# One array for a batch's attention inputs, turned memory summaries for batch 0, weight steps ahead of the last softmax steps

## The chip, the cores and the metric

The kernel runs on one core of a Trainium2 chip. The metric is the device time of one launch in microseconds (us); the time before is the median of three runs. A profiled execution gives the trace that is read here. Its engines are TensorE (PE for products, PEld for weight loads), VectorE (DVE), ScalarE (ACT), GpSimd (POOL) and SyncE (SP, which issues most of the loads).

## The reference

Three stages follow each other, all in float32:

- attention through memories, for 4 batches and 8 heads: with phi [576, 32] a softmax of phi over the 576 positions gives `a`; the summaries are `k_m = a^T k` and `v_m = a^T v` (32 x 64 each); then `softmax(q k_m^T / 8) v_m` over the 32 memories;
- a gated layer on the 2304 tokens of width 512: `(silu(x w_gate) * (x w_val)) w_out`, with 1536 inner columns;
- a layer of 8 experts with noisy top-2 routing and 1024 inner columns each.

The change touches the first stage for batch 0 (its input layout for all batches) and the first steps of the second stage.

## The kernel before

The program is one hand-ordered instruction stream for each engine (`manual_schedule`). Each engine runs its own instructions in the order in which the code names them and waits where its operands aren't there. The 2304 tokens are worked in 8 blocks of 288; a batch is two blocks. The 1536 inner columns of the second stage are 12 columns of 128, and a slot (`slot1`, or `slot0` for block 0) does one column of one block: gate and value products (`gv`, L436), the gate on VectorE (`gate_act`), the product back (`down`).

What comes before the first slot is the front. It is written out call by call (L735 to L776) for batch 0, in two halves of four heads each (`g` = 0, 1):

- `s1_a`, `s1_e`, `s1_r` (L248 to L260): maximum of phi, exponential with its sum, reciprocal of the sum (`st[:, 2]`).
- `s1_b`, `s1_bc` (L264 to L279): PE turns the exponentials in chunks of 128 positions (six transposes), ScalarE copies them to `en`.
- `s1_c` (L281): 20 calls of P.matmul for one summary, k or v of one half: five chunks by four heads, each head with an output of 32 memories by 64, the four on different output rows. `s1_cv` scales by the reciprocal, `s1_d` turns the result with PE, `s1_dc` copies it to `KM`.
- `s2_first` (L333): the first scores of one half and VectorE's 32x32 transposes of them; `s2_a` (maximum, subtract), `s2_e` (exponential, ScalarE), `s2_b` (sum, reciprocal, multiply, transpose), `s2_c` and `s2_d` (x's high part on ScalarE, its low part on VectorE).
- The second stage's weights come in thirds of 512 KB (`wa`). `top(n)` on ScalarE and `low(n)` on VectorE unpack third `n`, and `low` frees a buffer, for which SP then issues another load (L196). Thirds 0 and 1 are gate and value of column 0.
- The v summary is not applied to each token. `proj_a`, `proj_h`, `proj_b` (L397 to L413) multiply it into the weights of a column instead: PE's product, its high part on ScalarE, its low part on VectorE. `gv` multiplies high by high, low by high and high by low, for both halves: six products for the gate and six for the value.

SP's loads of the front stand in one queue: phi (two), k of half 0, q, k of half 1, v of both halves, then the thirds in the order of their use. PSUM tiles for small results take turns over six banks (`other`, L96).

Of the kernel before, what the change touches and what calls it, by code (L numbers as in the profile page):

```python
# [1 line left out]

# [57 lines left out]
OUT_ROWS = T + CAP  # L60


def r(ap):
    return ap.bitcast(F32R)
# [3 lines left out]
def moe_program(ctx, tc, phi, kv, q, wa, wgn, nz, wb, out):  # L68
# [41 lines left out]

    def load_phi(b, g):
        t = att.tile([128, S], F32, tag="phi", name="phi", bufs=2)
        Q.dma_start(t, phi[2 * b + g])
        PH[b, g] = t

    def load_part(s):
        for g in range(2):
            if s == 0:
                if g:
                    load_q(0)  # L120
                    KV[0, 1] = wpool.tile([128, 4096], F32, tag="X1", name="kv", bufs=1)[:, :2 * ROW].rearrange(
                        "p (s w) -> p s w", s=2)
                else:
                    KV[0, 0] = att.tile([128, 2, ROW], F32, tag="kv", name="kv", bufs=1)
            Q.dma_start(KV[0, g][:, s], kv[g, :, s])

    def load_kv(b, g):
        KV[b, g] = att.tile([128, 2, ROW], F32, tag="kv", name="kv", bufs=1)
        Q.dma_start(KV[b, g], kv[2 * b + g])

    def load_q(i):
        QT[i] = att.tile([128, 4, BT], F32, tag="q", name="qt", bufs=1)
        Q.dma_start(QT[i], q[i].rearrange("p (q t) -> p q t", q=4))
# [71 lines left out]
    for s in range(2):  # L205
        load_part(s)
# [56 lines left out]

    def s1_b(b, g):  # L264
        e, st = ST[b, g]
        p = other([128, 4, 128], "pT")
        for c in range(4):
            P.transpose(p[:, c, :], e[:, 128 * c:128 * (c + 1)], ident)
        p2 = other([128, 128], "pT")
        P.transpose(p2, e[:, S - 128:S], ident)  # L270
        P.transpose(p2[:64], e[:, S - 64:S], ident)
        TP[b, g] = p, p2
# [8 lines left out]
    def s1_c(b, g, s=slice(0, 2)):  # L281

        en, st = ST[b, g]
        p = other([128, 2, D] if b else [128, D], "pkv")
        t = KV[b, g][:, s]
        for c in range(5):
            for h in range(4):
                o, d = (slice(0, 128), 4 * D * c + D * h) if c < 4 else (
                    slice(64 * (h // 2), 64 * (h // 2) + 64), 16 * D + D * (h % 2))
                P.matmul(p[32 * h:32 * h + 32], en[o, c, 32 * h:32 * h + 32], t[o, ..., d:d + D],  # L290
                         start=(c == 0), stop=(c == 4))
        TP[b, g, s if b == 0 else 2] = p

    def s1_cv(b, g, s=2, eng=None):
        st = ST[b, g][1]
        out = kz[g][:, :, g, :] if s == 2 else kz[g][:, s, g, :]
        p = TP.pop((b, g, s))
        if eng is None:
            V.tensor_scalar(out, p, st[:, 2:3], None, op0=OP.mult)
        else:  # L300
            A.activation(out, p, AF.Copy, scale=st[:, 2:3])

    def s1_d(b, g, s=2):

        p = other([128, 2, 128], "pT")
        for m in range(2):
            if s in (m, 2):
                P.transpose(p[:64 * g + 64, m, :], kz[g][:, m].rearrange("p n d -> p (n d)"), ident)
        TP[b, g, s] = p

    def s1_dc(b, g, s=2):
        if b not in KM:
            KM[b] = att.tile([128, 2, 4, M], F32, tag="km", name="km", bufs=2)
        o = slice(64 * g, 64 * g + 64)
        m = slice(0, 2) if s == 2 else slice(s, s + 1)
        A.activation(KM[b][o, m].rearrange("p s k m -> p s (k m)"), TP.pop((b, g, s))[o, m], AF.Copy)
# [118 lines left out]

    def gv(i, f):  # L436
        pg, pv = bank(4, [128, BT], "pg"), bank(5, [128, BT], "pv")
        for a, p in enumerate((pg, pv)):
            for g in range(2):
# [307 lines left out]
    s1_cv(0, 1, 0, A)  # L747
    s2_e(0, 0)
    s1_d(0, 1, 0)
    s1_dc(0, 1, 0)  # L750
# [24 lines left out]
    del spare[:]  # L775
    spare.extend([6, 7])  # L776
# [44 lines left out]
    def slot0(f):  # L821
        run(0, 2 * f)
        c = ((f,) if f < 2 else (0, 1),)
        if f % 2 == 0 or f == 1:
            for fn in (proj_a, proj_h, proj_b):
                fn(0, f // 2, *c)
# [4 lines left out]
        if f == 0:  # L831
            top(2)
# [619 lines left out]
def layout(inputs):  # L1452
# [6 lines left out]
    arrays["phi"] = a("phi").reshape(B, 4, 2, S, M).transpose(0, 2, 1, 4, 3).reshape(2 * B, 128, S)  # L1459
    kv = np.stack([a("k").reshape(B, 4, 2, S, D), a("v").reshape(B, 4, 2, S, D)], axis=4)  # L1460
    kv = kv.transpose(0, 2, 3, 4, 1, 5).reshape(2 * B, S, 2, 4 * D)
    tail = kv[:, 512:].reshape(2 * B, 64, 2, 2, 2 * D).transpose(0, 3, 1, 2, 4).reshape(2 * B, 128, 2, 2 * D)
    kv = kv[:, :512].reshape(2 * B, 4, 128, 2, 4 * D).transpose(0, 2, 3, 1, 4).reshape(2 * B, 128, 2, 16 * D)
    arrays["kv"] = np.concatenate([kv, tail], axis=-1)
    q = a("q").reshape(B, 4, 2, S, D).transpose(1, 2, 4, 0, 3).reshape(4, 128, NB, BT)
    arrays["q"] = q.transpose(2, 1, 0, 3).reshape(NB, 128, 4 * BT)
# [17 lines left out]
_ORDER = ["phi", "kv", "q", "wa", "wgn", "nz", "wb"]  # L1484
# [15 lines left out]
```

## Time and profile before

| | |
|---|---|
| runs before | 847.76, 848.74, 850.28 us (median 848.74) |
| profiled execution | 849.52 us, span 847.7 us from first to last instruction |
| mean granted TensorE clock | 0.987 |
| busy, share of the span | PE 822.0 us (97%), PEld 729.4 (86%), DVE 638.7 (75%), ACT 389.9 (46%), POOL 247.5 (29%) |
| HBM | 105.34 MB read, 36.68 MB written, 168 GB/s over the span |

The span is the time between the first and the last instruction of the trace; the profiled execution's own time has 1.8 us around it. Engine busy time leaves out instructions that only wait, branch or issue a load. The granted clock is what the throttle allowed TensorE, as a share of 2.4 GHz; 0.50 is the lower of its two levels.

### The profile page before, as it was taken

Reading aid. Unit: us, or ns where it says so; the run is one execution under the profiler, and the core shown is the slowest. Engines: PE = TensorE matmul, PEld = TensorE weight load, DVE = VectorE, ACT = ScalarE, POOL = GpSimd, SP = SyncE. Lnnn points to the kernel's source line nnn. Section 1 sums busy time; section 2 is a strip of 40 time slices with the busy share of each in tenths; the row PEclk is TensorE's granted clock in tenths of the full one; section 3 lists DMA queues with packets and bytes.
Section 4 is the critical chain, followed back from the end, with each engine's and each line's share of the span. In section 5 each row is a group of like instructions: output and inputs, shape, how many; then the busy total and the mean of one; then the engine's idle time right before and its main releaser. Section 6 shows DMA issues by size and latency. Waiting matters only on the chain. (4 is left out here: it accounts for less than half of the span.)

```text
span 847.7 us, 16453 instructions
## 1 busy us (share of the span) xinstructions
PE 822.0 (97%) x6224; PEld 729.4 (86%) x6224; DVE 638.7 (75%) x1532; ACT 389.9 (46%) x804; POOL 247.5 (29%) x347
## 2 busy tenths in 40 slices
PE   5899999999999999999999999999999999999996
PEld 3678888899989998989899988888888888888885
DVE  4788497675867577777685587798889988899771
ACT  4665565333443334333445455445446464454430
POOL 2000012424333242443122143322414324054232
PEclk8799999999999999999999999999999999999999
DMA  9983838884426363446946993635574645654521
GB/s 341 402 328 125 254 98 303 262 279 131 124 51 214 99 207 98 131 112 145 272 151 222 211 254 73 136 111 115 138 172 87 161 116 119 163 117 108 182 82 64
DMA packets 78280, 143.18 MB, mean 169 GB/s; under 512 B 16080, under 2 KB 36784, under 8 KB 77424
## 3 DMA queue, kind: packets, MB, share of 16 engines
q1 hardware_dynamic: 58832, 100.66, 38.2%
q0 software_dynamic: 19360, 41.38, 20.1%
q8 instruction: 51, 0.84, 0.4%
q14 instruction: 37, 0.30, 0.1%
HBM read 105.34 MB, written 36.68 MB: 168 GB/s over the span
## 5 line engine op out<-in xcount | busy, mean ns | idle before, releaser
L1144 PE MATMUL acc<-ws,hs 128*128 128x512 f32 (+1 forms) x690 | 174.9, 394 | 0.0
L1130 PEld LDWEIGHTS ph<-xh,ws 128*128 128x128 f32 x1008 | 150.9, 188 | 11.0 <-DVE y L1170 0.8
L1130 PE MATMUL ph<-xh,ws 128*128 128x308 f32 x1008 | 157.6, 304 | 1.3 <-DVE y L1170 0.6
L1144 PEld LDWEIGHTS acc<-ws,hs 128*128 128x128 f32 (+1 forms) x690 | 122.7, 184 | 24.4
L985 POOL DMA_INDIRECT out<-pv,ix x40 | 64.2, 1606 | 179.9 <-ACT pv L977 70.8
L474 PE MATMUL acc<-a,ro 128*128 128x288 f32 x576 | 116.4, 295 | 0.0
L441 PE MATMUL pg<-x,pt 128*128 128x288 f32 x576 | 103.2, 314 | 4.4 <-DVE ta L454 2.3
L474 PE MATMUL acc<-a,os 128*128 128x288 f32 x432 | 105.8, 294 | 0.8 <-DVE os L423 0.8
L441 PEld LDWEIGHTS pg<-x,pt 128*128 128x128 f32 x576 | 82.1, 191 | 24.1 <-issue 6.8
L441 PE MATMUL pv<-x,pt 128*128 128x288 f32 x576 | 93.3, 298 | 0.0
L474 PEld LDWEIGHTS acc<-a,ro 128*128 128x128 f32 x576 | 92.1, 188 | 0.0
L441 PEld LDWEIGHTS pv<-x,pt 128*128 128x128 f32 x576 | 83.1, 191 | 0.0
L454 DVE SCALAR_TENSOR_TENSOR ta<-ta,pg 128x288 f32<-128x288 f32 x84 | 37.8, 450 | 60.1 <-ACT ta L449 60.1
L638 POOL DMA_INDIRECT xs<-R,gidx x48 | 48.2, 1004 | 112.6 <-DMA xs<-R,gidx 95.0
L474 PEld LDWEIGHTS acc<-a,os 128*128 128x128 f32 x432 | 74.1, 188 | 1.1 <-DVE os L423 1.1
L449 ACT ACTIVATE ta<-pg 128x288 f32<-128x288 f32 x84 | 34.4, 409 | 80.1 <-PE pg L441 80.1
L460 ACT ACTIVATE a<-ta 128x288 fp32r<-128x288 f32 x84 | 37.3, 444 | 70.6 <-DVE ta L455 66.9
L433 POOL DMA_DIRECT2D os<-osl x72 | 40.7, 567 | 93.5 <-PE acc L474 50.2
L942 PE MATMUL ph<-xt,wm 128*128 128x384 f32 (+1 forms) x256 | 55.6, 307 | 0.9 <-DVE xt L904 0.9
L942 PEld LDWEIGHTS ph<-xt,wm 128*128 128x128 f32 x256 | 43.8, 189 | 3.7 <-DVE xt L904 1.1
L455 DVE TENSOR_TENSOR ta<-ta,pv 128x288 f32<-128x288 f32 x84 | 38.2, 455 | 9.1 <-DVE ta L454 0.5
L461 DVE TENSOR_TENSOR a<-ta,a 128x288 fp32r<-128x288 f32 x84 | 37.5, 446 | 5.3 <-ACT a L460 4.9
(234 smaller groups left out, 1442.1 us busy)
## 6 DMA issues: line engine op xcount, KB each, us to landing
wb<-wb SPq DMA_DIRECT2D x70, 512.0 KB, 4.5
os<-osl POOLq DMA_DIRECT2D x72, 256.0 KB
kv<-kv SPq DMA_DIRECT2D x6, 1152.0 KB, 9.2
xl<-xs SPq DMA_DIRECT2D x40, 160.0 KB, 6.4
stg<-wa SPq DMA_DIRECT2D x12, 511.8 KB, 8.3
out<-zt SPq DMA_DIRECT2D x1, 5888.0 KB
xd<-R SPq DMA_DIRECT2D x8, 603.0 KB
qt<-q SPq DMA_DIRECT2D x8, 576.0 KB, 6.7
```

The costliest lines, as they stand in the source:

```text
L433: G.dma_start(r(lo), r(osl[f][:, :]))
L441: P.matmul(p, r(PT[f // 2, g][:, w, f % 2, 128 * a:128 * a + 128]), r(X[i][:, s, g, :]), start=(g == 0 and n == 0), stop=(g == 1 and n == 2))
L454: V.scalar_tensor_tensor(ta, ta, 1.0, pg, op0=OP.add, op1=OP.mult)
L455: V.tensor_mul(ta, ta, pv)
L460: A.activation(r(ah[:, 0, :]), ta, AF.Copy)
L461: V.tensor_sub(r(ah[:, 1, :]), ta, ah[:, 0, :])
L474: P.matmul(ACC[i][c], r(OS[i, f][w][:, o]), r(ah[:, s, :]), start=(f == 0 and n == 0), stop=(f == NF1 - 1 and n == 2))
L638: G.indirect_dma_start(out=xs[:, :], out_offset=bass.IndirectOffsetOnAxis(ap=RT[i][:, t, n:n + 1], axis=0), in_=R[i][:, t, :], in_offset=None)
L942: P.matmul(p, r(w[:, c]), r(x[:, k, b, :]), start=(m == 0), stop=(m == 11))
L985: G.indirect_dma_start(out=out, out_offset=bass.IndirectOffsetOnAxis(ap=IX[e][:h, t:t + 1], axis=0), in_=PV[e, t][:h], in_offset=None, com ...
L1130: P.matmul(out, r(w[i][:, c + 128 * k:c + 128 * k + 128]), r(x[:, m, k, a]), start=(start and n == 0), stop=(n == 5), skip_group_check=not ...
L1144: P.matmul(AC2[e, t][:h], r(a[:, n, o]), r(w[b][:, n]), start=(f == 0 and m == 0), stop=(f == NF2 - 1 and m == 2))
```

## The change

All of a batch's attention inputs lie in one array, `xin`, block after block in the order in which batch 0 loads them, each block contiguous over its 128 partitions. Later batches load k and v of a half by two loads. For batch 0 the reciprocal is multiplied into an identity (`dg`), and plain products with it turn and scale the exponentials in one step; `turned` then computes a summary directly in its turned form, 64 output rows (the width of a head) by 32 memories, two heads at a time side by side, and copies it to `KM` on ScalarE; the scale, PE's second transposes and their copies are gone for batch 0. The order of the front is written anew: the unpacking of thirds 0 to 2 and column 0's projection stand ahead of the last softmax steps, and x's low parts come last. The first gate and value products of block 0 take x's low part last (`FEW`). Block 0's softmax result of half 1 gets a place of its own in the tile that holds `dg`.

```diff
+PLACE, LONG = {}, 0
+for name, n in (("phi0", S), ("phi1", S), ("k0", 18 * D), ("q0", 4 * BT), ("k1", 18 * D), ("v0", 18 * D),
+                ("v1", 18 * D), ("q1", 4 * BT)):
+    PLACE[name] = LONG, n
+    LONG += 128 * n
...
+    def section(b, name):
+        o, n = PLACE[name]
+        return xin[b, o:o + 128 * n].rearrange("(p n) -> p n", n=n)
...
+    def load_part(b, g, s):
+        if (b, g) not in KV:
+            if b == 0 and g:
+                KV[b, g] = wpool.tile([128, 4096], F32, tag="X1", name="kv", bufs=1)[:, :2 * ROW].rearrange(
+                    "p (s w) -> p s w", s=2)
+            else:
+                KV[b, g] = att.tile([128, 2, ROW], F32, tag="kv", name="kv", bufs=1)
+        Q.dma_start(KV[b, g][:, s], section(b, f"{'kv'[s]}{g}"))
     def load_kv(b, g):
-        KV[b, g] = att.tile([128, 2, ROW], F32, tag="kv", name="kv", bufs=1)
-        Q.dma_start(KV[b, g], kv[2 * b + g])
+        for s in range(2):
+            load_part(b, g, s)
...
     load_phi(0, 1)
-    for s in range(2):
-        load_part(s)
+    load_part(0, 0, 0)
+    load_q(0)
+    for g, s in ((1, 0), (0, 1), (1, 1)):
+        load_part(0, g, s)
...
     def s1_b(b, g):
         e, st = ST[b, g]
+        if b:
+            turn = partial(P.transpose, identity=ident)
+        else:
+            if not EX:
+                EX.append(gpool.tile([128, 2, 2, BT], F32, tag="x", name="ex"))
+            dg = EX[0][:, 0, g, :128]
+            V.tensor_scalar(dg, ident, st[:, 2:3], None, op0=OP.mult)
+            turn = partial(P.matmul, rhs=dg, start=True, stop=True)
         p = other([128, 4, 128], "pT")
         for c in range(4):
-            P.transpose(p[:, c, :], e[:, 128 * c:128 * (c + 1)], ident)
+            turn(p[:, c, :], e[:, 128 * c:128 * (c + 1)])
         p2 = other([128, 128], "pT")
-        P.transpose(p2, e[:, S - 128:S], ident)
-        P.transpose(p2[:64], e[:, S - 64:S], ident)
+        turn(p2, e[:, S - 128:S])
+        turn(p2[:64], e[:, S - 64:S])
         TP[b, g] = p, p2
...
+    def turned(g, s):
+        en = ST[0, g][0]
+        z = slice(64 * g, 64 * g + 64)
+        for m in range(2):
+            p = other([128, 64], "pkv")
+            for n in range(2):
+                for c in range(5):
+                    o, d = (slice(0, 128), 4 * D * c + D * (2 * m + n)) if c < 4 else (
+                        slice(64 * m, 64 * m + 64), 16 * D + D * n)
+                    h = 64 * m + 32 * n
+                    P.matmul(p[z, 32 * n:32 * n + 32], KV[0, g][o, s, d:d + D], en[o, c, h:h + 32],
+                             start=(c == 0), stop=(c == 4))
+            A.activation(memory(0)[z, s, 64 * m:64 * m + 64], p[z], AF.Copy)
...
-        at = att.tile([128, BT], F32, tag="at", name="at")
+        at = att.tile([128, BT], F32, tag="at", name="at") if i or not g else EX[0][:, 1, 0, :]
...
+    ALL = [(w, s, g) for g in range(2) for w, s in ((0, 0), (0, 1), (1, 0))]
+    FEW = [(w, s, g) for w, s in ((0, 0), (1, 0), (0, 1)) for g in range(2)]
     def gv(i, f):
         pg, pv = bank(4, [128, BT], "pg"), bank(5, [128, BT], "pv")
         for a, p in enumerate((pg, pv)):
-            for g in range(2):
-                for n, (w, s) in enumerate(((0, 0), (0, 1), (1, 0))):
-                    P.matmul(p, r(PT[f // 2, g][:, w, f % 2, 128 * a:128 * a + 128]), r(X[i][:, s, g, :]),
-                             start=(g == 0 and n == 0), stop=(g == 1 and n == 2))
+            for n, (w, s, g) in enumerate(FEW if i == f == 0 else ALL):
+                P.matmul(p, r(PT[f // 2, g][:, w, f % 2, 128 * a:128 * a + 128]), r(X[i][:, s, g, :]),
+                         start=(n == 0), stop=(n == 5))
...
-    for fn in (s1_a, s1_e, s1_r):
+    for fn in (s1_a, s1_e):
         both(fn, 0)
     for g in range(2):
+        s1_r(0, g)
         s1_b(0, g)
         s1_bc(0, g)
-    s1_c(0, 0, 0)
-    s1_cv(0, 0, 0)
-    s1_d(0, 0, 0)
-    s1_dc(0, 0, 0)
+    turned(0, 0)
     s2_first(0)
     s2_a(0, 0)
-    s1_c(0, 1, 0)
-    s1_cv(0, 1, 0, A)
+    turned(1, 0)
     s2_e(0, 0)
-    s1_d(0, 1, 0)
-    s1_dc(0, 1, 0)
     s2_b(0, 0)
     s2_first(1)
     s2_a(0, 1)
-    s1_c(0, 0, 1)
-    s1_cv(0, 0, 1, A)
-    s1_d(0, 0, 1)
+    top(0)
+    low(0)
+    turned(0, 1)
     s2_c(0, 0)
-    s1_dc(0, 0, 1)
-    s2_d(0, 0)
-    s2_e(0, 1)
-    s1_c(0, 1, 1)
-    s1_cv(0, 1, 1, A)
-    s1_d(0, 1, 1)
-    s1_dc(0, 1, 1)
-    top(0)
-    s2_b(0, 1)
-    low(0)
-    s2_c(0, 1)
     top(1)
     low(1)
-    s2_d(0, 1)
+    s2_e(0, 1)
+    turned(1, 1)
     places(True)
+    del spare[:]
+    spare.extend([6, 7])
+    proj_a(0, 0, (0,))
+    top(2)
+    proj_h(0, 0, (0,))
+    s2_b(0, 1)
+    s2_c(0, 1)
+    proj_b(0, 0, (0,))
+    both(s2_d, 0)
...
-        if f % 2 == 0 or f == 1:
+        if f and f % 2 == 0 or f == 1:
...
-        if f == 0:
-            top(2)
```

## Rows read from the trace of the kernel before

**Rows 1.** The page: span, and 40 slices: PE's busy tenths, granted clock's tenths.

```profile
span 847.7 us, 16453 instructions
...
PE   5899999999999999999999999999999999999996
...
PEclk8799999999999999999999999999999999999999
```

**Rows 2.** Windows: stretch, length, busy (count) PE PEld DVE ACT POOL, clock, DMA, GB/s.

```profile
5.00:10.00 5.00, 4.27 (x52) 3.40 (x52) 0.80 (x6) 2.49 (x8) 0.63 (x1) 1.00 0.98 336
...
10.00:15.00 5.00, 3.25 (x58) 1.25 (x58) 2.83 (x8) 1.30 (x4) 0.00 (x0) 0.82 1.02 415
...
20.00:25.00 5.00, 1.95 (x19) 1.10 (x20) 2.51 (x5) 2.95 (x7) 0.00 (x0) 0.50 1.02 407
...
30.00:35.00 5.00, 5.00 (x47) 3.43 (x46) 3.22 (x7) 3.12 (x6) 0.00 (x0) 0.63 1.04 407
```

**Rows 3.** Order of time, first summaries: start, length, engine, line, operation, out<-in, count, [idle].

```profile
1.27 0.23 DVE L216 TENSOR_SCALAR ident<-jp 128x128 f32<-128x128 int32 x1 [1.27 <-POOL warm L220]
...
5.25 1.12 PE L268 MATMUL pT<-ident,phi 128*128 128x128 f32 x4 [5.25 <-ACT phi L255]
...
5.41 0.16 DVE L260 RECIPROCAL st<-st 128x1 f32<-128x1 f32 x1
...
8.33 1.45 PE L290 MATMUL pkv<-kv,en 128*32 128x64 f32 x40 [0.26 <-ACT en L277]
...
9.34 0.20 PEld L290 LDWEIGHTS pkv<-kv,en 64*32 64x32 f32 x8 [0.17 <-issue]
...
10.53 0.27 ACT L316 ACTIVATE km<-pT 64x128 f32<-64x128 f32 x1 [2.08 <-PE pT L308]
...
10.85 0.69 PE L326 MATMUL psc<-qt,km 64*32 64x288 f32 x8 [0.36 <-ACT km L316]
...
11.47 0.90 PE L290 MATMUL pkv<-kv,en 128*32 128x64 f32 x40
```

**Rows 4.** Order of time, VectorE's softmax of block 0.

```profile
11.60 0.48 DVE L338 STREAM_TRANSPOSE sm<-psc 128x288 f32<-128x288 f32 x1 [1.47 <-PE psc L326]
...
13.58 0.45 DVE L360 TENSOR_REDUCE rd<-sm 128x9 f32<-128x288 f32 x1 [0.51 <-ACT sm L355]
...
15.41 0.44 DVE L338 STREAM_TRANSPOSE sm<-psc 128x288 f32<-128x288 f32 x1
...
17.98 0.45 DVE L360 TENSOR_REDUCE rd<-sm 128x9 f32<-128x288 f32 x1 [0.33 <-ACT sm L355]
...
20.75 0.69 DVE L198 SCALAR_TENSOR_TENSOR wa<-stg,top 128x512 int32<-128x512 int32 x1 [0.85 <-ACT top L194]
...
22.31 0.45 DVE L374 TENSOR_TENSOR x<-at,x 128x288 fp32r<-128x288 f32 x1
```

**Rows 5.** Order of time, the first projections and gate products.

```profile
22.54 1.11 PE L326 MATMUL pp<-wa,km 64*32 64x256 f32 x16 [2.94 <-DVE wa L198]
...
24.14 0.76 DVE L413 TENSOR_TENSOR pt<-pp,pt 128x256 fp32r<-128x256 f32 x2 [1.38 <-ACT pt L408]
...
24.16 1.81 PE L441 MATMUL pg<-x,pt 128*128 128x288 f32 x6 [0.51 <-ACT pt L408]
...
25.08 1.32 DVE L198 SCALAR_TENSOR_TENSOR wa<-stg,top 128x512 int32<-128x512 int32 x2 [0.18 <-ACT top L194]
...
27.34 1.11 PE L326 MATMUL pp<-wa,km 64*32 64x256 f32 x16
...
35.73 1.17 PE L441 MATMUL pg<-x,pt 128*128 128x288 f32 x6
```

**Rows 6.** Order of time, loads of late thirds and their use.

```profile
41.22 2.20 SPq L167 DMA_DIRECT2D stx<-wa  x3
...
55.05 1.39 ACT L194 ACTIVATE top<-stx 128x512 f16<-128x512 bf16 x2
```

**Rows 7.** The tile `stx`, issues to 43.1 us: load's issue to landing.

```profile
DMA to landing us min/median/max: 9.3/9.8/10.3
```

More of the change, by code (lines that the diff above doesn't have):

```diff
@@ L1 @@
 from contextlib import ExitStack
+from functools import partial
 import concourse.bass as bass
@@ L67, in moe_program @@
 @with_exitstack
-def moe_program(ctx, tc, phi, kv, q, wa, wgn, nz, wb, out):
+def moe_program(ctx, tc, xin, wa, wgn, nz, wb, out):
     nc = tc.nc
@@ L109, in moe_program @@
     ROW = 18 * D
+    def section(b, name):
+        o, n = PLACE[name]
+        return xin[b, o:o + 128 * n].rearrange("(p n) -> p n", n=n)
     def load_phi(b, g):
         t = att.tile([128, S], F32, tag="phi", name="phi", bufs=2)
-        Q.dma_start(t, phi[2 * b + g])
+        Q.dma_start(t, section(b, f"phi{g}"))
         PH[b, g] = t
-    def load_part(s):
-        for g in range(2):
[L118 to L125, printed above, removed]
+    def load_part(b, g, s):
[6 more added lines that the diff above has]
+        Q.dma_start(KV[b, g][:, s], section(b, f"{'kv'[s]}{g}"))
     def load_kv(b, g):
-        KV[b, g] = att.tile([128, 2, ROW], F32, tag="kv", name="kv", bufs=1)
-        Q.dma_start(KV[b, g], kv[2 * b + g])
+        for s in range(2):
+            load_part(b, g, s)
     def load_q(i):
         QT[i] = att.tile([128, 4, BT], F32, tag="q", name="qt", bufs=1)
-        Q.dma_start(QT[i], q[i].rearrange("p (q t) -> p q t", q=4))
+        Q.dma_start(QT[i], section(i // 2, f"q{i % 2}").rearrange("p (q t) -> p q t", q=4))
     ORDER = [(0, 0), (0, 1), (1, 0), (1, 1)]
@@ L279, in s1_bc, with s1_c @@
         ST[b, g] = (en, ST[b, g][1])
-    def s1_c(b, g, s=slice(0, 2)):
+    def s1_c(b, g):
         en, st = ST[b, g]
-        p = other([128, 2, D] if b else [128, D], "pkv")
-        t = KV[b, g][:, s]
+        p = other([128, 2, D], "pkv")
         for c in range(5):
@@ L289, in s1_c, with s1_cv @@
                     slice(64 * (h // 2), 64 * (h // 2) + 64), 16 * D + D * (h % 2))
-                P.matmul(p[32 * h:32 * h + 32], en[o, c, 32 * h:32 * h + 32], t[o, ..., d:d + D],
+                P.matmul(p[32 * h:32 * h + 32], en[o, c, 32 * h:32 * h + 32], KV[b, g][o, :, d:d + D],
                          start=(c == 0), stop=(c == 4))
-        TP[b, g, s if b == 0 else 2] = p
-    def s1_cv(b, g, s=2, eng=None):
+        TP[b, g] = p
+    def s1_cv(b, g):
         st = ST[b, g][1]
[L296 to L301, printed above, removed]
@@ L303, in s1_d @@
-    def s1_d(b, g, s=2):
+        V.tensor_scalar(kz[g][:, :, g, :], TP.pop((b, g)), st[:, 2:3], None, op0=OP.mult)
+    def s1_d(b, g):
         p = other([128, 2, 128], "pT")
         for m in range(2):
[L307 to L311, printed above, removed]
+            P.transpose(p[:64 * g + 64, m, :], kz[g][:, m].rearrange("p n d -> p (n d)"), ident)
+        TP[b, g] = p
@@ L312, in s1_dc, with memory @@
+    def memory(b):
         if b not in KM:
             KM[b] = att.tile([128, 2, 4, M], F32, tag="km", name="km", bufs=2)
+        return KM[b].rearrange("p s k m -> p s (k m)")
+    def s1_dc(b, g):
         o = slice(64 * g, 64 * g + 64)
-        m = slice(0, 2) if s == 2 else slice(s, s + 1)
-        A.activation(KM[b][o, m].rearrange("p s k m -> p s (k m)"), TP.pop((b, g, s))[o, m], AF.Copy)
+        A.activation(memory(b)[o], TP.pop((b, g))[o], AF.Copy)
+    def turned(g, s):
[11 more added lines that the diff above has]
+            A.activation(memory(0)[z, s, 64 * m:64 * m + 64], p[z], AF.Copy)
@@ L438, in gv @@
         for a, p in enumerate((pg, pv)):
-            for g in range(2):
-                for n, (w, s) in enumerate(((0, 0), (0, 1), (1, 0))):
-                    P.matmul(p, r(PT[f // 2, g][:, w, f % 2, 128 * a:128 * a + 128]), r(X[i][:, s, g, :]),
-                             start=(g == 0 and n == 0), stop=(g == 1 and n == 2))
+            for n, (w, s, g) in enumerate(FEW if i == f == 0 else ALL):
+                P.matmul(p, r(PT[f // 2, g][:, w, f % 2, 128 * a:128 * a + 128]), r(X[i][:, s, g, :]),
+                         start=(n == 0), stop=(n == 5))
         tag = ("ah", "al")[f % 2]
@@ L1458, in layout @@
     arrays = {}
-    arrays["phi"] = a("phi").reshape(B, 4, 2, S, M).transpose(0, 2, 1, 4, 3).reshape(2 * B, 128, S)
+    phi = a("phi").reshape(B, 4, 2, S, M).transpose(0, 2, 1, 4, 3).reshape(B, 2, 128, S)
     kv = np.stack([a("k").reshape(B, 4, 2, S, D), a("v").reshape(B, 4, 2, S, D)], axis=4)
[L1461 to L1466, printed above, removed]
+    kv = kv.transpose(0, 2, 3, 4, 1, 5).reshape(B, 2, S, 2, 4 * D)
+    tail = kv[:, :, 512:].reshape(B, 2, 64, 2, 2, 2 * D).transpose(0, 1, 4, 2, 3, 5).reshape(B, 2, 128, 2, 2 * D)
+    kv = kv[:, :, :512].reshape(B, 2, 4, 128, 2, 4 * D).transpose(0, 1, 3, 4, 2, 5).reshape(B, 2, 128, 2, 16 * D)
+    kv = np.concatenate([kv, tail], axis=-1)
+    q = a("q").reshape(B, 4, 2, S, D).transpose(1, 2, 4, 0, 3).reshape(4, 128, B, 2, BT)
+    q = q.transpose(2, 3, 1, 0, 4)
+    parts = {f"phi{g}": phi[:, g] for g in range(2)}
+    for g in range(2):
+        parts |= {f"k{g}": kv[:, g, :, 0], f"v{g}": kv[:, g, :, 1], f"q{g}": q[:, g]}
+    arrays["xin"] = np.concatenate([parts[n].reshape(B, -1) for n in PLACE], axis=1)
     def up(w):
@@ L1481, in layout @@
     return arrays
-_ORDER = ["phi", "kv", "q", "wa", "wgn", "nz", "wb"]
+_ORDER = ["xin", "wa", "wgn", "nz", "wb"]
 def kernel(**inputs):
```

3 lines of the change are left out of this document (1 added, 2 removed).

## The prediction

> **What bounds the kernel now.** I read the page's slices first. From the second slice (21.2 us each) PE is at 9 tenths or more to the last, at the upper clock level of 2.4 GHz; only the first two slices have PE at 5 and 8 tenths and the granted clock at 8 and 7 tenths [rows 1]. So TensorE bounds the whole but the first 35 us, and the new layout, the turned summaries and the moved steps all act there, but for one: later batches' k and v come as two loads instead of one. Whatever the front gains or loses reaches the end if nothing later takes it back.
>
> Then the windows of the front. PE is busy 3.25 of 5 us in 10:15 and 1.95 of 5 in 20:25, with the clock falling to 0.50 [rows 2]. The view in order of time says why. The column reads 1.00 in 5:10, but the same 40 products of L290 take 1.45 us at 8.33 and 0.90 at 11.47: up to about 10 us PE ran at the lower level (1.2 GHz), then shortly at the upper, and at the lower again from 13.2 to 33.7 (the means 0.82 in 10:15 and 0.63 in 30:35 put the changes there) [rows 2, 3].
>
> The chain itself: the exponentials of phi, the phi transposes, batch 0's four summaries, the first scores at 10.85 [rows 3], then VectorE's softmax [rows 4]. After the second softmax ends VectorE stands 0.85 us waiting for the first weight third's top half, because its two weight steps stand behind the softmax; PE stands 2.94 us at 22.54 waiting for those steps, and the first gate product starts at 24.16 [rows 4, 5]. The next projection, at 27.34, I use as the finish of the front: from there both kernels issue the same work in the same order.
>
> **The change part by part.** *Layout.* Batch 0's blocks come in the same order and sizes, only contiguous. I cost it at nothing: in the changed kernel PE is still on the scaled transposes when the first k was needed before (8.33), so an earlier k is not used. If k came later than 10.5, all would move one for one. The six later k/v loads become twelve of half the size, 82 us or later, when rows 1 show PE full: nothing.
>
> *Scaled transposes.* L268 was one instruction per chunk, 1.12 us for four with the drain, so 0.21 us of spacing at the lower level (128 columns) [rows 3]. The change makes them plain products with a scaled identity. A plain fp32 product is two instructions (L290 has 40 for 20 calls), so 12 calls are 24 instructions of 0.21: 5.1 us against 2.6 at the lower level. They also start later: the reciprocal of the first half's sum ends at 5.57, the scaled identity takes 0.23 like the 128x128 identity at 1.27 [rows 3], and a hand-over 0.05: 5.85 instead of 5.25, with nothing queued behind on PE that could have run. PE has been at work for some 4 us when the level rises near 10 in the kernel before; I let it rise there too. By 10.0, 19 or 20 are issued, the rest take 0.11 each: done at 10.5.
>
> *Turned summaries.* Each of the four replaces 40 products of 64 columns that run four abreast (one per head, 32 output rows each) by 40 of 32 columns that write the same 64 rows and so can't run abreast. Four abreast took (1.45 - 0.3)/10 = 0.11 us a round at the lower level and 0.06 at the upper. Alone and half as wide, 0.055 and 0.03. Forty: 2.2 or 1.2 us. The tail chunk, which uses half of the rows, cost 0.17 us of loader idle once per summary [rows 3]; now it comes in four times and goes out three, 7 x 0.17 = 1.2 at the lower level, about 0.6 at the upper. With a drain of 0.2: 2.0 us at the upper level against 0.90, 3.6 at the lower against 1.45. Bounds for one, upper level: 0.9 (as now) to 7 x 0.17 + 40 x 0.06 = 3.6. I take 2.0, which lies nearer to L290's own spacing. What goes: per summary a scale, a transpose and its hand-overs. The first summary's products ended at 9.78 and its copy started at 10.53 [rows 3]; now the copy follows the products at once, so 0.75 less, and each copy is two of 64 columns (0.22 each from 0.27 for 128), the first hidden under the second half's products.
>
> So the first scores: 10.5 + 2.0 + 0.3 (copy, hand-over) + 0.69 = 13.5, against 11.54. The front's first half *loses* 2.0 us.
>
> *The reordered steps.* From there VectorE is never without work, so I add its steps in the new order: transpose, max, subtract and the wait for the exponential 13.58 - 11.60 = 1.98; tail of softmax 15.41 - 13.58 = 1.83; second head 1.98 - 0.51 = 1.47; two weight steps 2 x 0.69 = 1.38, under which the second exponential now hides; second tail 1.83; low part of the projection 0.76; two low parts of x, 0.90; next two weight steps 1.32 [rows 4, 5]. Sum 11.5, with hand-overs 11.6: the low parts of x end at 13.5 + 11.6 - 1.3 = 23.8, the weight steps at 25.1. The first projection itself (1.11 us) needs only the first two weight steps (13.5 + 1.98 + 1.83 + 1.47 + 1.38 = 20.2) and the last summary, and is no longer waited for: of the 2.94 us nothing is left on the path. What queues behind the moved steps: ScalarE's two weight copies (0.78 each) stand ahead of the second exponential, at about 15.6 and 18.8, when their thirds have landed (they are read now at 19.94 with no wait for a load); SP's reload for the freed buffer only joins a queue that is already full (407 to 415 GB/s) [rows 2].
>
> The gate product now does the products with x's low part last, so it can start near 22 and is left with one of six at 23.8; then six value products. At the lower level, 1.81 - 0.4 of drain over six is 0.24 each [rows 5]: 23.8 + 0.1 + 7 x 0.24 = 25.6. The next projection starts there: 25.6 against 27.34, **1.75 us less**; with the clock still up, 25.1 and 2.2 less. I take 1.9. Behind it the work is the same at the same level: one gate/value pair, a projection, and then the clock rises after the dense work, as at 33.7; both move with the start.
>
> Does the rest keep it? The weights could take it back. The thirds issued at 41.22 land after 9.3 us, 50.5, and are read at 55.05: 4.5 us to spare, more than 1.9 [rows 6, 7]. With PE full from there on, I carry all.
>
> The profiled execution took 849.52 us for a span of 847.7. 849.52 - 1.9 = 847.6; it was 0.8 above the median of the runs (848.74), so against that median 846.8.
>
> **The rivals.** *The clock stays down.* If those narrow products don't lift the level, PE is the bound and not VectorE: transposes to 11.0; four summaries of 3.4 (2.2 + 1.2), 13.6; two scores of 1.1 and the copies before them and before the projection, 0.5 each, 3.7: the projection can start at 28.3 and ends at 29.4. Its high part (0.7), the last x copy (0.4), the low parts (1.2) and seven products of 0.24 follow: 33.4 against 27.34, 6.1 **slower**, 854.8. For it: the third and fourth summaries did not lift the level, 0.50 in 20:25 [rows 2]. Against: PE now has almost no gaps from 5.9 to 20, where it had 1.75 of 5 us idle in 10:15, and the level did rise at 10. The same count at the upper level puts PE last from summaries of 2.0 us on. 12 in 100.
>
> *The clock holds through the first gate products.* From 24.16 to the rise at 33.7 PE works 9.5 us at the lower level, 3.2 a gate/value pair (27.34 - 24.16); at the upper a gate product's six take 1.17 for 1.81 [rows 5], so all of it some 6.0. VectorE is busy 3.22 of 5 us there [rows 2] and must finish its steps between the pairs, so I allow 2.5 of the 3.5: with the 1.9, 844.4. Against: PE is thin for some 3 us before the first gate product, and it was a thinner 10:13 that dropped it. 17 in 100.
>
> *Transposes don't count.* The rows: the level rose within 2.5 us of the first plain product (8.33, upper by 10.85) after 2.8 us of transposes [rows 3]. If only plain products lift it, the new front, plain from 5.85, has the upper level at 8.4 and not 10: 1.6 us at double speed, 0.8 more: 846.0. Nothing in the rows tells the two apart. 10 in 100. The Trainium skill, TensorE: Matmul & The Clock Gate, Part 4: PE-mode transpose, says that transposes are not counted as PE work for the clock; by that rule the time is this rival's.
>
> *The longer front eats the order's gain.* Summaries of 2.5 us at the upper level put PE last by 4 x 0.5 = 2.0, and nothing is left: 848.7, no change; one of my bounds for a summary, 3.6, lies beyond. 16 in 100.
>
> **How the numbers follow.** Forecast 45 in 100, its own range 845.4 to 848. 0.3% is 2.5 us, about what a measurement of this kernel can tell from none: faster means under 846.2, slower over 851.3. Faster: a quarter of the forecast case (11), all of the clock that holds (17), six of the ten of the transposes, and 3 of the rest: 37. Slower: the first rival, less the case that the level rises late in the front, 11. Within: 52. Range: from the clock that holds to a little way towards the slower rival, 844 to 850.5.
>
> **What would show it.** First scores near 13.5, and VectorE without a gap from there to 25; L290's successor at 2 us a summary; the 0.85 and 2.94 waits gone; the projection of the second column at 25.6; the same wait-free PE after 35. Wrong if the summaries take 2.5 us or more, if the granted clock is at 0.50 all through 10:24, or if the first k lands after 10.5.

## The result and the profile after

The changed kernel takes 860.82 us (median of five runs, 857.21 to 863.12) against 849.44 (847.76 to 851.38, five runs): ratio 1.0141, interval 1.0121 to 1.0161, 11.4 us slower. The forecast was 846.8 with a range to 850.5. The profiled execution, 857.21 us, is the shortest of the five.

The page of the changed kernel: span, busy time, and the granted clock in tenths by slices of 21.4 us.

```profile
span 855.4 us, 16483 instructions
...
PE 835.4 (98%) x6232; PEld 742.6 (87%) x6232; DVE 637.5 (75%) x1533; ACT 389.6 (46%) x805; POOL 243.9 (29%) x347
...
PEclk9699999999999999999999999999999999999999
```

PE is busier than before, 835.4 us for 822.0, and in the clock only the front differs: its first two slices read 9 and 6 tenths where they read 8 and 7 [rows 1].

TensorE in order of time, changed kernel (start, time of the group, line, tiles, shapes, count, idle time ahead and its releaser). L288 are the scaled transposes, L344 the turned summaries, L356 scores and projections, L473 gate and value. The last two rows are narrow windows: ten and nine neighbouring products of a summary at the upper and at the lower clock level (the shape named is that of the first of them, a tail chunk with half of the input rows).

```profile
6.18 2.05 PE L288 MATMUL pT<-ex,phi 128*128 128x128 f32 x8 [6.18 <-ACT phi L265]
...
11.44 3.26 PE L344 MATMUL pkv<-en,kv 128*64 128x32 f32 x40
14.63 1.05 PE L356 MATMUL psc<-qt,km 64*32 64x288 f32 x8
15.61 4.23 PE L344 MATMUL pkv<-en,kv 128*64 128x32 f32 x40
19.77 1.55 PE L356 MATMUL psc<-qt,km 64*32 64x288 f32 x8
21.25 10.79 PE L344 MATMUL pkv<-en,kv 128*64 128x32 f32 x80
31.98 1.48 PE L356 MATMUL pp<-wa,km 64*32 64x256 f32 x16
33.97 2.17 PE L473 MATMUL pg<-x,pt 128*128 128x288 f32 x6 [0.51 <-ACT pt L438]
...
37.51 0.82 PE L356 MATMUL pp<-wa,km 64*32 64x256 f32 x16
...
12.78 0.88 PE L344 MATMUL pkv<-en,kv 64*64 64x32 f32 x10
...
25.05 1.28 PE L344 MATMUL pkv<-en,kv 64*64 64x32 f32 x9
```

A summary that took 0.90 or 1.45 us [rows 3] takes 3.26 at the upper level and 5.4 (10.79 for two) at the lower. From 11.4 to 33.5 us PE has no gap: it bounds the front alone. The second column's projection starts at 37.51, where it started at 27.34 [rows 5].

VectorE in the same view: it waits three times for work that stands behind PE's summaries (L380 to L395 are the softmax, L206 the weight step, L443 the projection's low part).

```profile
15.73 0.48 DVE L368 STREAM_TRANSPOSE sm<-psc 128x288 f32<-128x288 f32 x1 [8.93 <-PE psc L356]
...
20.60 0.45 DVE L390 TENSOR_REDUCE rd<-sm 128x9 f32<-128x288 f32 x1 [3.40 <-ACT sm L385]
...
27.97 0.69 DVE L206 SCALAR_TENSOR_TENSOR wa<-stg,top 128x512 int32<-128x512 int32 x1 [3.51 <-ACT top L202]
...
33.95 0.76 DVE L443 TENSOR_TENSOR pt<-pp,pt 128x256 fp32r<-128x256 f32 x2 [3.46 <-ACT pt L438]
```

ScalarE is named as the releaser, but its exponential and unpacking stand behind copies of summaries that it could not make yet: it waited 16.2 us in all, eight times, for PE's summaries.

Windows of the changed kernel (stretch, its length, busy time and count of PE, PEld, DVE, ACT, POOL, granted clock, DMA share, GB/s):

```profile
15.00:20.00 5.00, 5.00 (x50) 4.07 (x48) 1.40 (x3) 0.34 (x2) 0.00 (x0) 0.74 1.03 414
20.00:25.00 5.00, 5.00 (x37) 3.61 (x34) 3.66 (x9) 1.44 (x4) 0.00 (x0) 0.50 1.02 408
25.00:30.00 5.00, 5.00 (x39) 4.55 (x40) 1.90 (x5) 1.72 (x5) 0.00 (x0) 0.50 1.03 409
```

PE is busy without a gap and still at the lower level (1.2 GHz); before, the level fell in a stretch with gaps [rows 2]. The clock's records put the rise at 10.61, the fall at 17.44 and the next rise at 37.92, behind the first gate and value products.

**Where the difference stands.** In both kernels ScalarE's step on the gate product of block 0's last column comes at the end of the same work: 75.57 us before, 84.97 after. The same difference, 9.4 us to a tenth, still stands at 372 us. From 400 to 530 us VectorE waits in the third stage for loads by index (xl from xs) that take another time in every run, and there the profiled executions drift by -1.9 to +6.4 us against the kernel before. The table gives both for all kernels (the others are described below): the front's difference, read at that step of one profiled execution, and the ratio of the timed runs.

| kernel | front, us | ratio | interval |
|---|---|---|---|
| the change | +9.40 | 1.0141 | 1.0121 to 1.0161 |
| layout_only | -0.10 | 0.9991 | 0.9970 to 1.0011 |
| order_old | -3.58 | 0.9975 | 0.9953 to 0.9997 |
| scaled_only | +1.53 | 1.0034 | 1.0016 to 1.0052 |
| turned_only | +12.59 | 1.0156 | 1.0124 to 1.0189 |
| wide_moving | +4.16 | 1.0052 | 1.0025 to 1.0080 |
| narrow_weights | -0.17 | 1.0026 | 1.0006 to 1.0046 |
| abreast | +0.55 | 0.9992 | 0.9972 to 1.0011 |
| prescaled | +11.16 | 1.0130 | 1.0091 to 1.0169 |
| split | +3.59 | 1.0042 | 1.0025 to 1.0060 |
| split_prescaled | +0.35 | 1.0028 | 1.0008 to 1.0049 |
| order_best | -1.77 | 0.9971 | 0.9951 to 0.9990 |

### The profile page after: what moved, and what is told of

Read it like the earlier page. It is cut to its first block, busy times and chain, and to the rows that moved or that the text cites. A ratio compares the mean times of both kernels' runs of the same rounds, so it can differ in the third digit from the quotient of the medians.

```text
span 855.4 us, 16483 instructions
## 1 busy us (share of the span) xinstructions
PE 835.4 (98%) x6232; PEld 742.6 (87%) x6232; DVE 637.5 (75%) x1533; ACT 389.6 (46%) x805; POOL 243.9 (29%) x347
## 5 line engine op out<-in xcount | busy, mean ns | idle before, releaser
L1007 POOL DMA_INDIRECT out<-pv,ix x40 | 61.7, 1542 | 178.7 <-ACT pv L999 70.5
L473 PE MATMUL pg<-x,pt 128*128 128x288 f32 x576 | 102.9, 313 | 3.8 <-DVE ta L486 2.1
L473 PEld LDWEIGHTS pg<-x,pt 128*128 128x128 f32 x576 | 81.6, 190 | 23.4 <-issue 6.0
L473 PE MATMUL pv<-x,pt 128*128 128x288 f32 x576 | 92.6, 296 | 0.0
L473 PEld LDWEIGHTS pv<-x,pt 128*128 128x128 f32 x576 | 82.4, 189 | 0.0
```

Of the source, the lines that this page charges most:

```text
L1007: G.indirect_dma_start(out=out, out_offset=bass.IndirectOffsetOnAxis(ap=IX[e][:h, t:t + 1], axis=0), in_=PV[e, t][:h], in_offset=None, com ...
```

## The experiments, one part at a time

**order_old: layout and new order, with the old summaries.**

```diff
-    turned(0, 0)
+    s1_c(0, 0, 0)
+    s1_cv(0, 0, 0)
+    s1_d(0, 0, 0)
+    s1_dc(0, 0, 0)
...
```

> The change's layout and its new order of steps, with batch 0's summaries computed as before (plain transposes, 32 output rows a head, scale, second transpose). Theory S (the turned summaries are the loss: a narrow product costs 0.107 us at the lower level and 0.058 at the upper, not 0.055 and 0.03): the first scores stay near 10.85, VectorE's steps follow in the new order, the second column's projection comes near 25 us against 27.3 before, 845.5 to 848.5 us. Rival O (the new order is the loss): that projection after 33 us, 855 us or more. Rival L (the layout is the loss): first k later than 9.5 us, 852 or more.

TensorE in order of time:

```profile
18.97 1.53 PE L337 MATMUL pp<-wa,km 64*32 64x256 f32 x16
21.02 2.17 PE L454 MATMUL pg<-x,pt 128*128 128x288 f32 x6 [0.51 <-ACT pt L419]
...
24.56 1.11 PE L337 MATMUL pp<-wa,km 64*32 64x256 f32 x16
```

The new order gains: 24.56 for 27.34, and 3.6 us at the front's end. Part of the 3.6 may be the clock and not the order: in this execution the level rose for the rest of the front at 25.97, in the kernel before at 33.70. order_best (below) keeps this order with two more moves; there the level rose at 31.53 and the front gained 1.8. The runs of order_old show 0.25% (2.1 us). The profiled execution loses some 4 us against the kernel before between 396 and 412, to one such load by index (VectorE's row below): PE stood still for 3.35 us and had the lower level for 3.4 us behind it. Whether that is chance or comes of arriving earlier was not tried.

```profile
403.56 0.58 DVE L913 STREAM_TRANSPOSE xu<-xl 128x384 f32<-128x384 f32 x1 [4.67 <-DMA xl<-xs]
```

**layout_only: the input array alone.**

```diff
-        Q.dma_start(t, phi[2 * b + g])
+        Q.dma_start(t, section(b, f"phi{g}"))
...
```

> The kernel before with the one array xin alone. S and O: 847.5 to 850.5 us, the same as before, the first k landing at the same 8.2 us. L: slower by 4 us or more, 853 up.

The front's first column stands where it stood (projections at 22.60 and 27.40), and the ratio holds 1. The layout is worth nothing here.

**scaled_only: the kernel before with the scaled, plain transposes; the old summaries leave their scale out.**

```diff
+            V.tensor_scalar(dg, ident, st[:, 2:3], None, op0=OP.mult)
+            turn = partial(P.matmul, rhs=dg, start=True, stop=True)
...
-            V.tensor_scalar(out, p, st[:, 2:3], None, op0=OP.mult)
+            V.tensor_scalar(out, p, 1.0 if b == 0 else st[:, 2:3], None, op0=OP.mult)
```

> The kernel before with the scaled identity in plain products in place of batch 0's phi transposes; the summaries then need no scale but are computed as before. S: the transposes end near 11.5 us and not 8.1, all behind them 3 us later, 851 to 853 us. Rival T (the scaled transposes are the main loss): the projection of the second column after 34 us, 857 or more. If the products lift the clock earlier and hold it: 848 to 850.

```profile
12.95 0.90 PE L301 MATMUL pkv<-kv,en 128*32 128x64 f32 x40
...
14.86 0.69 PE L337 MATMUL psc<-qt,km 64*32 64x288 f32 x8 [0.36 <-ACT km L327]
...
30.11 0.66 PE L337 MATMUL pp<-wa,km 64*32 64x256 f32 x16
```

First scores at 14.86 for 10.85, second column's projection at 30.11 for 27.34: of the 4.0 us at the first scores 2.8 are left there and 1.5 at the front's end. The transposes, expected to end near 11.5, ended at 13: PE began them at 6.87, and the level rose only at 12.97. This step alone costs 0.34%.

**turned_only: before's layout and order, with scaled transposes and turned summaries.**

```diff
-    s1_c(0, 0, 0)
-    s1_cv(0, 0, 0)
-    s1_d(0, 0, 0)
-    s1_dc(0, 0, 0)
+    turned(0, 0)
...
```

> The kernel before with scaled transposes and turned summaries, in the old order and layout. S: as slow as the change or slower, since the new order gains and is missing: 860 to 865 us; the 40 products of a summary take 3.2 to 5.4 us. T: not more than 2 us over the run with the scaled transposes alone. O: 850 to 854.

```profile
12.00 3.26 PE L335 MATMUL pkv<-en,kv 128*64 128x32 f32 x40
...
22.06 10.79 PE L335 MATMUL pkv<-en,kv 128*64 128x32 f32 x80
...
40.45 1.10 PE L347 MATMUL pp<-wa,km 64*32 64x256 f32 x16
```

The summaries take the same 3.26 and 10.79 as in the whole change. From scaled_only to here the front grows by 11.1 us. So the turned summaries carry the loss, the scaled transposes some 1.5 to 3 us, and the order takes 3.2 back (12.59 here, 9.40 in the whole change).

## The experiments on the turned summaries

Two things were open: what sets the pitch (the time from one product's start to the next one's) of products with 64 weight columns and 32 moving columns, and why the clock fell while PE was never idle. Ten neighbouring products, read in a narrow window, make the pitches comparable.

**wide_moving: each product moves 64 columns instead of 32** (the other 32 are not used).

```diff
-                    P.matmul(p[z, 32 * n:32 * n + 32], KV[0, g][o, s, d:d + D], en[o, c, h:h + 32],
+                    P.matmul(p[z, n, :], KV[0, g][o, s, d:d + D], en[o, c, 64 * m:64 * m + 64],
...
```

> The changed kernel, but each product of a turned summary moves 64 columns (both heads of its pair) instead of 32; half of each result is not used. In the changed kernel the products stand 0.0585 us apart at the upper clock level and 0.107 at the lower. Three readings of that. In series: a product's weight load (64 columns) and its pass (32) follow each other because they use the same columns of the array, so 64 moving columns give about 0.083 and 0.16: a summary of 4.3 us at the upper level, 6 to 8 us more in all. Load: the load of 64 weight columns alone sets the pitch, so 0.058 and 0.107 as in the changed kernel, and the time stays within 3 us of it. Floor: no product takes less than 64 columns' time, the same numbers as Load. A separate question is the clock: if the lower level from 17.4 us on came from narrow passes, twice the columns would hold the upper level longer, and the time could come out 3 to 6 us lower than the changed kernel although it computes more.

```profile
12.60 0.93 PE L343 MATMUL pkv<-en,kv 64*64 64x64 f32 x10
...
12.04 3.47 PE L343 MATMUL pkv<-en,kv 128*64 128x64 f32 x40
...
20.96 6.98 PE L343 MATMUL pkv<-en,kv 128*64 128x64 f32 x80
...
32.34 0.67 PE L356 MATMUL pp<-wa,km 64*32 64x256 f32 x16
```

Twice the moving columns take 0.93 us for ten where the changed kernel took 0.88; the starts stand 0.058 to 0.059 apart in both. So the moving columns did not set the pitch, and load and pass do not stand in series. And the clock never fell in this front (two summaries in 6.98 at 20.96, where the changed kernel needed 10.79): 5.2 us less of front and 854.08 for 860.82, by computing twice as much per product (and one more small copy a pair). The mean granted clock of the timed runs points the same way, 0.994 to 0.999 in these ten and 0.981 to 0.987 in the changed kernel's five; it is a weak sign, since a stretch ahead of the first record counts as full speed (prescaled, below, reads 0.996).

**narrow_weights: 32 weight columns instead of 64, the same 32 moving columns.** Half of batch 0's summary rows are not computed (they are filled by a second copy).

```diff
-                    P.matmul(p[z, 32 * n:32 * n + 32], KV[0, g][o, s, d:d + D], en[o, c, h:h + 32],
+                    P.matmul(p[64 * g:64 * g + 32, 32 * n:32 * n + 32], KV[0, g][o, s, d:d + 32], en[o, c, h:h + 32],
...
```

> The changed kernel, but each product of a turned summary loads 32 weight columns (half of a head's width) instead of 64, with the same 32 moving columns; the other half of the summary's rows is not computed (the rows are filled by a second copy), so half of batch 0's summaries is left out. In series: 0.045 us upper and 0.08 lower per product, a summary of 2.5 us at the upper level; the time about 4 us less than the changed kernel. Load: 0.03 and 0.053, the spacing that the prediction had, a summary near 2.0 us; then the whole time should come near the prediction's (847 to 851). Floor: 0.058 and 0.107 unchanged, and the time that of the changed kernel.

```profile
12.47 0.61 PE L344 MATMUL pkv<-en,kv 64*32 64x32 f32 x10
...
12.10 2.21 PE L344 MATMUL pkv<-en,kv 128*32 128x32 f32 x39
...
18.86 4.42 PE L344 MATMUL pkv<-en,kv 128*32 128x32 f32 x80
...
28.02 0.67 PE L357 MATMUL pp<-wa,km 64*32 64x256 f32 x16
```

The pitch falls to 0.032, a summary to 2.2 us, the level holds, and the front is that of the kernel before. The weight width set the pitch; a floor at 64 columns' time for any product is refuted. The time, 852.40, is 1.4 us above the expected 847 to 851; its profiled execution stands 0.7 us ahead of the kernel before at 470 and 3.6 behind it at 505, with VectorE held 6.2 us by one load by index in between.

**abreast: the two halves' products alternate** (output rows 0 to 63, then 64 to 127).

```diff
+                    for g in range(2):
...
+                        P.matmul(p[64 * g:64 * g + 64, 32 * n:32 * n + 32], KV[0, g][o, s, d:d + D],
+                                 ST[0, g][0][o, c, h:h + 32], start=(c == 0), stop=(c == 4))
```

> The changed kernel, but the two halves' turned products alternate (half 0 writes output rows 0 to 63, half 1 rows 64 to 127), so that two neighbours use different columns of the array; both k summaries stand together ahead of the first scores, both v summaries behind half 0's x. If the spacing comes from load and pass in the same columns (In series), or from a floor per group of columns, neighbours overlap and the spacing halves to about 0.03 and 0.055: two summaries in some 3.5 us at the upper level, first scores no later than in the changed kernel, the time 850 to 853. If one loader sets the pitch (Load), or the floor is for the whole array, 0.058 and 0.107 stay: the first scores come 3 to 4 us later and the time is that of the changed kernel or up to 3 us above.

```profile
13.69 0.90 PE L343 MATMUL pkv<-en,kv 64*64 64x32 f32 x20
...
12.23 3.41 PE L343 MATMUL pkv<-en,kv 128*64 128x32 f32 x80
...
23.18 1.11 PE L355 MATMUL pp<-wa,km 64*32 64x256 f32 x16 [3.22 <-DVE wa L206]
...
28.41 1.08 PE L355 MATMUL pp<-wa,km 64*32 64x256 f32 x16
```

Twenty products in the time of ten: weight loads for different output rows do go side by side, so the part of Load that has one loader for all is refuted. The first scores came at 15.57, 0.9 later than in the changed kernel, against what was expected, because both k summaries stand ahead of them. VectorE then bounds the front (PE waits 3.22), and the time is that of the kernel before: 0.9992.

The Trainium skill, TensorE: Matmul & The Clock Gate, section LDWEIGHTS (loading the stationary operand), prices a weight load by its columns alone, columns / 1.2 in ns; by that an estimate for 64 is 0.053 us. The upper level's 0.058 is near it, the lower level's 0.107 is twice that. The same page's section The mechanism (packing small matmuls) says that a load overlaps running products only where the input rows differ, and names a background weight buffer as another way; here both halves use all 128 input rows and only their output rows differ, and they overlap. Which way the chip took no run shows.

**split: each product as two of 32 weight columns, on neighbouring output rows** (nothing left out).

```diff
+                    for q in range(2):
+                        P.matmul(p[64 * g + 32 * q:64 * g + 32 * q + 32, 32 * n:32 * n + 32],
+                                 KV[0, g][o, s, d + 32 * q:d + 32 * q + 32], en[o, c, h:h + 32],
...
```

> The changed kernel, with each product of a turned summary issued as two products of 32 weight columns each, on output rows 0 to 31 and 32 to 63 of its half (80 products a summary, nothing left out). If the pitch is set by the longer of a product's two widths (weight columns, moving columns) in its own 32 output rows, and products on other rows run beside it, a pair takes what one narrow product took, 0.032 us at the upper clock level: a summary near 2.2 us, the level held from its rise on, second column's projection at 28, the front 0 to 0.5 us from the kernel before, the time 849 to 852. If products on other rows do not run beside each other in the turned form (one loader for all), each piece adds 0.032: a summary as in the changed kernel, and the time within 3 us of 860.8, or 854 if the level holds.

```profile
12.03 0.63 PE L345 MATMUL pkv<-en,kv 64*32 64x32 f32 x20
...
11.10 2.26 PE L345 MATMUL pkv<-en,kv 128*32 128x32 f32 x78
...
24.52 0.62 PE L345 MATMUL pkv<-en,kv 128*32 128x32 f32 x10 [2.50 <-issue]
...
30.67 1.11 PE L358 MATMUL pp<-wa,km 64*32 64x256 f32 x16
```

The pitch rule holds: a pair in 0.032, the whole summary in 2.26. The time did not follow: PE stood still for 2.50 us within the last summary, from 22.02 to 24.52, waiting for nothing that the profile shows, the clock fell at 23.34, and the front came to +3.59 where 0 to 0.5 was expected. The trace's DMA packets give a hint: a 16 KB transfer in the queue of kind "instruction" (q8) starts at 21.95, 6.2 us after the one before, and takes 1.03 us. narrow_weights, with half of these products, has its transfers at 18.73 and 27.58, and no such gap. So PE may have waited for its own instructions; that was not tried.

**prescaled: the exponentials scaled on VectorE, one transpose instruction each.**

```diff
...
-            dg = EX[0][:, 0, g, :128]
-            V.tensor_scalar(dg, ident, st[:, 2:3], None, op0=OP.mult)
-            turn = partial(P.matmul, rhs=dg, start=True, stop=True)
...
+            V.tensor_scalar(e, e, st[:, 2:3], None, op0=OP.mult)
+        turn = partial(P.transpose, identity=ident)
```

> The changed kernel, but the exponentials of batch 0 are scaled by the reciprocal on VectorE (one instruction of 576 columns per half, about 0.7 us by the estimate, of which the first stands on the path) and PE turns them by one transpose instruction each, as before. The PE cost of the scaled transposes (12 instructions more, 2.6 us at the lower level) goes. If the scaled transposes' share of the loss is what the kernel with them alone showed (0.34%), the time falls by about 2 us to 858 to 859; if the summaries' clock level or the number of PE's products is what decides later, it stays within 1 us of the changed kernel. Does the level rise later because transposes do not count? Plain products in the changed kernel begin at 6.18 us and the level rises at 10.1; here the first plain product comes at about 9: if transposes do not count for the level, it rises near 12 to 13 us, otherwise near 10.

```profile
9.33 5.43 PE L341 MATMUL pkv<-en,kv 128*64 128x32 f32 x40
...
23.01 10.79 PE L341 MATMUL pkv<-en,kv 128*64 128x32 f32 x80
...
39.27 0.85 PE L353 MATMUL pp<-wa,km 64*32 64x256 f32 x16
```

A miss: 862.11, not 858 to 859. PE began its summaries 2.1 us earlier and ran every product from 9.33 to 33.7 at the lower level. The first rise on record is at 39.73: 24 us of these products and the scores, without a gap, did not raise the level. (The expectation's 10.1 for the rise in the changed kernel is 10.61 by the records.)

**split_prescaled: both edits.**

```diff
+            V.tensor_scalar(e, e, st[:, 2:3], None, op0=OP.mult)
...
+                    for q in range(2):
...
```

> As the kernel with the split products, but the exponentials are scaled on VectorE and turned by one transpose each (as in the kernel of that name before). PE is through with the transposes at 9.4 instead of some 12 us, so the first scores come up to 2 us earlier if the clock level rises by 12 us, and the time is 1 to 2 us below the split kernel: 847 to 850. If without the dense plain transposes the level stays down, as it did with 64 by 32 products, a split summary takes about 3.2 us (0.053 a pair and the tail changes), four of them put PE last, and the time is 852 to 856.

```profile
8.84 0.42 PE L288 MATMUL pT<-ident,phi 128*64 128x128 f32 x1
9.19 2.27 PE L342 MATMUL pkv<-en,kv 128*32 128x32 f32 x78
...
23.04 1.11 PE L355 MATMUL pp<-wa,km 64*32 64x256 f32 x16 [2.49 <-DVE ex L394]
```

PE did nothing but transposes from 6.44 us, at the lower level, and the first summary, from 9.19 on, runs wholly at the upper (2.27, as in split): the level rose at 9.22. So the level rose here behind nothing but transposes; in prescaled the same transposes, 6.58 to 9.4, had no rise behind them. By the Trainium skill, TensorE: Matmul & The Clock Gate, Part 4: PE-mode transpose, they would not count; this row is against that. First scores at 11.25, 3.4 us earlier than in the changed kernel. Then PE stands still for 2.49 us, from 20.55 to 23.04. The row names VectorE, but that step ended at 22.15, and what the projection reads was there by 20.82 (ScalarE's last copy of a summary). It looks like the stop of split again: an instruction transfer starts at 20.41, and PE goes on 2.6 us later, as it did there. The time is 852.56, 2.6 above the expected range's upper end.

**order_best: order_old with both v summaries ahead of their turning and third 1 unpacked earlier.**

```diff
+    s1_c(0, 0, 1)
+    s1_c(0, 1, 1)
+    s1_cv(0, 0, 1, A)
     top(0)
     low(0)
-    s1_c(0, 0, 1)
-    s1_cv(0, 0, 1, A)
...
+    s1_cv(0, 1, 1, A)
     top(1)
     low(1)
```

> The kernel before with the new layout and the new order alone, its old summaries, and two more moves: both v summaries' products stand together ahead of their turning, and ScalarE unpacks third 1 ahead of the second softmax's exponential, the copies of the memories and x's high part. In the kernel with the new order alone PE waited 1.11 us for ScalarE's scale of a v summary at 16.30 and VectorE 0.84 us for third 1's top half at 18.06. If these two decide, the second column's projection starts 0.5 to 1 us earlier than the 24.56 there, and the ratio to the kernel before goes from 0.9975 to about 0.9965 (847 us). If the scale, the copies and the unpacking on ScalarE only trade places, it stays at 0.9975.

```profile
15.80 2.83 PE L301 MATMUL pkv<-kv,en 128*32 128x64 f32 x80
18.57 0.98 PE L319 MATMUL pT<-ident,kz 128*64 128x128 f32 x2
20.55 1.11 PE L337 MATMUL pp<-wa,km 64*32 64x256 f32 x16 [1.01 <-ACT sm L366]
...
25.97 1.11 PE L337 MATMUL pp<-wa,km 64*32 64x256 f32 x16
```

0.9971 (0.9951 to 0.9990): faster than the kernel before, not to be told from order_old's 0.9975. PE's wait of 1.11 us is gone, but ScalarE's later exponential now holds the projection for 1.01, and the second column's projection came at 25.97, later than order_old's 24.56 and not 0.5 to 1 us earlier. In this execution the level did not rise before 31.53, so the profile does not show whether the moves helped. These two are the versions whose interval lies below 1: faster than the kernel before by 0.3%, and than the change.

## Why the prediction was wrong

The step that failed is one term: "Alone and half as wide, 0.055 and 0.03". It took the old round's 0.11 and 0.06 [rows 3] as the time of 64 moving columns and halved it with them. But a turned product carries 64 weight columns where the old one carried 32. Four shapes show the rule at the upper level: 32 weights by 64 moving, 0.056 for a round of four (order_old, the four starting 0.007 apart); 64 by 32, 0.058; 64 by 64, 0.058; 32 by 32, 0.032. In these four the longer of the two widths sets the pitch within the same output rows. Turning a product swaps the widths and leaves their maximum, and what ran four abreast now runs alone: forty times 0.058 or 0.107. The upper bound of the prediction, 3.6 us, had used this pitch; the value taken, 2.0, used the half.

By its steps:

- *Layout, nothing*: right.
- *Scaled transposes done at 10.5*: they ended near 11.5. The count was right, but the start was 6.18 (5.85 forecast), the first half's twelve took 0.25 each (3.02 us to 9.20), and the level rose at 10.61 and not at 10.
- *Tail changes, 0.6 and 1.2 us a summary*: starts around a tail stand 0.153, 0.079, 0.149 and 0.079 apart instead of 0.058, 0.23 more each time, four times: 0.9 at the upper level; the same sum at the lower gives 1.1.
- *A summary of 2.0 us*: 40 x 0.058 + 0.9 = 3.2; 3.26 measured. At the lower level 40 x 0.107 + 1.1 = 5.4 for 3.6.
- *First scores end at 13.5*: 15.7.
- *"VectorE is never without work"*: false; it waited 3.40 + 3.51 + 3.46 = 10.4 us, all of it behind PE. This follows from the summary: past 2.0 us PE was last, as the prediction's own rival said.
- *The order's gain*: right in kind; that its size came near may be luck. The forecast had the longer front at 2.0 lost and 1.9 gained net, so 3.9 for the order; order_old's front shows 3.6, with an early rise of the clock in it, order_best's 1.8 without, and order_old's runs 2.1.
- *Second column's projection at 25.6*: 37.51.
- *The rest carries it*: right, to 372 us. (One reading on the way was off: PE is at 9 tenths from the third slice on, not from the second, and at 6 in the last [rows 1].)

The second half of the loss is the clock. The forecast counted on the upper level for the gap-free PE from 10 us on; the rows show it fall at 17.44 in the changed kernel and at 17.61 in turned_only, 6 us into these products, and not rise at all in prescaled until 39.73. With 64 moving columns (wide_moving), 32 weight columns (narrow_weights), or two products at a time (abreast, split), it held until PE stood idle. The split of the 9.4 us, from one profiled execution of each kernel: 5.2 from the change to wide_moving (the level, pitch the same), 4.3 from wide_moving to narrow_weights (the pitch, level the same, half of the summary left out).

Of the rivals, *the clock stays down* named this half of the mechanism and got 12 in 100; prescaled shows it whole. Its 33.4 for the second column's projection came out as 37.51, since it too priced a summary at 3.4 for 5.4. *Transposes don't count* is refuted by split_prescaled, where the level rose behind transposes alone. *The longer front eats the order's gain* was right at the upper level: its sum with wide_moving's 3.47 for 2.0 is 4 x 1.47 - 1.9 = 4.0 us later than before, and wide_moving's front has 4.16.

Open: when the level first rises differs between executions of nearly the same front (8.9 us in order_old, 31.5 in order_best), and with it the front; why the loads by index in the third stage take another time in each run; and whether the stops of 2.5 us in split and split_prescaled are waits for instructions. Why the same stream held the level with 64 moving columns and not with 32 is not shown either; the rows show only that it did.

## What to carry to other kernels

Until a row says otherwise, price a small product by the wider of its weights and its moving columns, as these four shapes had it, and ask which output rows it shares with its neighbours: turning it round saves nothing, and giving up four abreast costs the whole factor. A PE without gaps is not a PE at the upper clock; read the granted clock of a stretch that already runs the shape in question, and if there is none, keep the lower level in the range. Where one unmeasured pitch is multiplied by 160 and a rival turns on it, the upper bound of that pitch belongs in the forecast's own range.

## What the runs showed of the hardware

- Doubling the moving columns of a 64-column product changed its pitch by nothing (0.058 us both) and made the kernel 6.7 us faster, 5.2 of them in a front where the upper level held.
- Products with different output rows overlap in load and pass alike: twenty in 0.90 us where ten took 0.88, the two of a pair starting 0.007 us apart.
- The level can fall with PE busy in every window (0.74 and then 0.50 from 15 to 30 us).
- The level rose at 9.22 in split_prescaled behind nothing but transposes (from 6.44).
- A load by index in the third stage held VectorE 4.67 us in one execution of order_old and 8.45 in one of wide_moving, the latter with PE idle 3.42 us and the clock down for 6.8 us behind it.
